# Top-k attention and two MLPs on one core: the mask of the scores as a PReLU on ScalarE

## The chip, the core and the metric

One core of a Trainium2 chip runs the whole program in one launch. The core has five engines that run side by side, each through its own list of instructions in the order in which they stand there: TensorE (PE in the profile; its weight loads are PEld), VectorE (DVE), ScalarE (ACT), GpSimd (POOL), and SyncE (SP), which issues most of the transfers. An instruction starts when those ahead of it on its engine are done with it and the semaphores that it waits for are set. The metric is the device time of one execution in microseconds (us).

## What is computed

Attention over 2 x 8 heads with 576 positions of 64 elements, in which each query keeps its 32 largest scores, and behind it two MLPs over the 1152 tokens. Cut to what matters:

```python
scores = scale * np.matmul(q, k.transpose(0, 1, 3, 2))
kth = np.partition(scores, -top_k, axis=-1)[..., -top_k:-top_k + 1]   # top_k = 32
scores = np.where(scores >= kth, scores, -1000000000.0)
scores = scores - np.max(scores, axis=-1, keepdims=True)
attn = np.exp(scores)
attn = attn / (np.sum(attn, axis=-1, keepdims=True) + 1e-09)
x = np.matmul(attn, v)            # then (tokens, 512)
h = x @ w_in;  x = (h * tanh(softplus(h))) @ w_out      # MLP 1, 512 -> 2048 -> 512
h = x @ w_in2; x = (relu(h) ** 2) @ w_out2              # MLP 2
```

## The kernel before

The tokens go through in four rounds (`ROUNDS`) of 256, 320, 320 and 256. A round's attention is made for four pairs of heads, in tiles of 128 queries by 576 keys; there are 72 such tiles. While a later round's attention runs, TensorE does the MLPs of an earlier one in the places that are left.

A tile (`tile_of`) goes over the engines in turn. TensorE makes the scores, ScalarE copies them to `s`. VectorE finds the 32nd largest of each row (lines 477 to 482): a MAX8 gives the eight largest, MATCH_REPLACE8 strikes them out into `w`, and this is done until four groups of eight are found in `mx`. Then comes the mask: GpSimd makes `e` = -3e38 where a score is below the 32nd largest, else 0 (line 491), and adds `s` to it (line 493). ScalarE makes the bias `nm` (line 492) and takes the exponential of `e`, whose row sum it leaves in `acc`. TensorE transposes `e`, ScalarE copies that to `pt`. Two tiles (the two heads of a pair) or one make a unit. At a unit's end (`unit_end`, lines 529 to 536) the sums get a small constant on ScalarE, VectorE takes the reciprocal (line 531), and ScalarE spreads it to `r` (line 534). When all units of a pair are there, TensorE multiplies with the values (`px`, line 556), and VectorE scales (line 584) into the round's `x1`, with which the round's MLPs begin.

Beside it run these: the weights are converted once (`convert`: two activations, one VectorE instruction at line 686, a transfer to DRAM as `kept`). In round 0 the MLPs take `kept` as it is (256 fp32 matmuls at line 774). In round 1 each of 32 pieces is split into a high and a low part: ScalarE casts, and GpSimd makes the low part with four subtractions (`wide`, line 260). Both are written to DRAM (`both`), from where rounds 2 and 3 take them. In rounds 1 to 3 every product is three matmuls, 768 instructions a round, and the activation `g` is split too (`gl`, line 253), on VectorE in round 1 and on GpSimd in rounds 2 and 3 (`GL = "gvggg"`). Round 0's and round 1's Mish shares ScalarE with the attention's exponentials, and a switch of function costs an ACT_TABLE_LOAD.

The order of each engine's instructions is not written out by hand. `Order` is a planner: every step of every process states its engine, its estimated time and a rank, and the planner lets the engine that comes free take the ready step of the lowest rank. What it decides is the program's order. So an estimate that changes moves instructions on all engines. A switch of the activation function has a price in the plan only where a step names its table, as the exponential and Mish do:

```python
        yield ("POOL", 1.0, 8, lambda: nc.gpsimd.tensor_scalar(out=e, in0=s, scalar1=mx[:, 3, 7:8], scalar2=LOWEST, op0=ALU.is_lt, op1=ALU.mult))
```

Here 1.0 is the estimated time in us and 8 the rank.

## Time and profile before

| | |
|---|---|
| median of 3 runs | 789.98 us (789.24 to 790.78) |
| the profiled execution | 789.56 us, of which the span of the profile is 787.4 us |
| busy, us (share of the span) | PE 657 (83%), PEld 578 (73%), DVE 483 (61%), ACT 482 (61%), POOL 449 (57%) |
| granted TensorE clock, mean | 0.93 of full speed |

The busy share is a mean over stages that have different limits. Up to about 143 us there is only attention and the conversion of weights, up to about 330 us round 0's MLPs run beside attention, up to about 567 us round 1's, and behind that TensorE has rounds 2 and 3 to itself. The views by stage say more than the table.

### The profile page before, as it was taken

The page shows a single profiled execution, that of the slowest core. Times are in us where ns is not written, and L with a number is a line of the kernel's source. Part 1 is how long each engine was busy: PE and PEld are TensorE (multiplying, and loading weights), DVE is VectorE, ACT ScalarE, POOL GpSimd, SP SyncE. Part 2 cuts the span into 40 slices and gives each one's busy share as a digit, 9 for nine tenths or more (in the row PEclk, how much of TensorE's full clock was granted, in tenths as well). Part 3 has the DMA queues.
Part 4 walks back from the last instruction along what each step waited for, and adds up shares of the span by engine and source line. Part 5 has one row for each costly group of instructions (what it writes and reads, how often), then busy time and mean ns, then how long its engine had stood idle before and what let it go on. Part 6 is the DMA issues. An engine that isn't in the chain of part 4 may idle for free.

```text
span 787.4 us, 11662 instructions
## 1 busy us (share of the span) xinstructions
PE 657.4 (83%) x4056; PEld 578.1 (73%) x4056; DVE 483.1 (61%) x889; ACT 481.7 (61%) x1015; POOL 449.2 (57%) x381
## 2 busy tenths in 40 slices
PE   5353554979996999797869789789899999999997
PEld 2242443767775887687668677678799999999997
DVE  3678999978986999999788879888200000100000
ACT  3677865799876984686785567874552073151550
POOL 2476567445535666979899899989642042041230
PEclk9997656999998999898999999999999999999999
DMA  7999921595999875566556565657888888889995
GB/s 200 281 372 268 323 66 32 206 350 174 351 320 354 261 250 157 182 216 255 192 218 206 191 206 215 263 201 269 291 282 313 288 294 288 311 323 357 369 354 202
DMA packets 95290, 201.83 MB, mean 256 GB/s; under 512 B 36352, under 2 KB 61440, under 8 KB 82944
## 3 DMA queue, kind: packets, MB, share of 16 engines
q1 hardware_dynamic: 94144, 200.83, 74.0%
q8 instruction: 32, 0.52, 0.3%
q10 hardware_dynamic: 1088, 0.26, 0.1%
q14 instruction: 26, 0.21, 0.1%
HBM read 146.01 MB, written 52.69 MB: 252 GB/s over the span
## 4 chain that ended last, share of the span: by engine, by line
PE 41%; POOL 17%; DMA 15%; DVE 12%; ACT 8%; issue 5%; SPq 1%; POOLq 0%; ACTq 0%
PE pm L774 32%; POOL wt L260 7%; POOL e L491 6%; DMA wt<-both 6%; DMA w<-kept 5%; DVE w L481 5%; DVE mx L482 4%; POOL e L493 3%; PE ps L464 3%; PE px L556 2%; DMA kept<-cu 2%; ACT L247 2%; PE pt L502 2%; DVE mx L478 1%; ACT e L247 1%
## 5 line engine op out<-in xcount | busy, mean ns | idle before, releaser
L491 POOL TENSOR_SCALAR e<-s,mx 128x576 f32<-128x576 f32 x72 | 163.1, 2267 | 115.8 <-DVE mx L482 82.3
L774 PE MATMUL pm<-gh,wt 128*128 128x320 f32 (+1 forms) x768 | 172.0, 308 | 3.3 <-ACT gh L247 1.5
L774 PE MATMUL pm<-xh,wt 128*128 128x320 f32 (+1 forms) x768 | 172.1, 310 | 2.8 <-DMA wt<-both 1.4
L482 DVE MAX8 mx<-w 128x8 f32<-128x576 f32 x216 | 164.4, 761 | 7.4
L774 PEld LDWEIGHTS pm<-xh,wt 128*128 128x128 f32 x768 | 130.7, 194 | 5.4 <-ACT h L247 2.2
L253 POOL TENSOR_TENSOR gl<-h,gh 128x320 fp32r<-128x320 f32 (+1 forms) x64 | 51.8, 809 | 144.8 <-ACT gh L247 110.2
L774 PEld LDWEIGHTS pm<-gh,wt 128*128 128x128 f32 x768 | 130.4, 193 | 5.4 <-DMA wt<-both 2.4
L774 PE MATMUL pm<-gl,wt 128*128 128x320 f32 (+1 forms) x384 | 117.5, 306 | 2.3 <-DVE gl L253 2.3
L774 PE MATMUL pm<-xl,wt 128*128 128x320 f32 (+1 forms) x384 | 117.5, 306 | 0.2
L481 DVE MATCH_REPLACE8 w<-mx,w 128x576 f32<-128x576 f32 x144 | 106.9, 742 | 0.0
L493 POOL TENSOR_TENSOR e<-s,e 128x576 f32<-128x576 f32 x72 | 104.0, 1447 | 3.8
L260 POOL TENSOR_TENSOR wt<-w,wt 128x256 fp32r<-128x256 f32 x128 | 94.6, 775 | 9.0 <-ACT wt L247 8.8
L502 PE MATMUL pt<-ident,e 128*128 128x128 f32 x288 | 53.0, 315 | 51.7 <-ACT e L247 41.1
L247 ACT ACTIVATE e<-e,nm 128x576 f32<-128x576 f32 x72 | 55.7, 774 | 66.0 <-POOL e L493 65.8
L502 PEld LDWEIGHTS pt<-ident,e 128*128 128x128 f32 x288 | 39.3, 160 | 61.8 <-ACT e L247 46.3
L774 PEld LDWEIGHTS pm<-gl,wt 128*128 128x128 f32 x384 | 74.2, 193 | 3.0 <-DVE gl L253 3.0
L774 PEld LDWEIGHTS pm<-xl,wt 128*128 128x128 f32 x384 | 74.7, 195 | 0.6 <-DVE xl L253 0.6
L247 ACT ACTIVATE h<-pm 128x320 f32<-128x320 f32 (+1 forms) x112 | 45.5, 413 | 46.4 <-PE pm L774 44.8
L955 DVE COPY ot<-pm 128x256 f32<-128x256 f32 x16 | 6.7, 421 | 101.9 <-PE pm L947 54.2
L253 DVE TENSOR_TENSOR xl<-pm,xh 128x320 fp32r<-128x320 f32 (+1 forms) x12 | 5.6, 468 | 101.7 <-ACT xh L247 101.5
L247 ACT ACTIVATE pt<-pt 128x640 f32<-128x640 f32 x72 | 50.4, 700 | 26.4 <-PE pt L504 25.9
L774 PE MATMUL pm<-gh,w 128*128 128x256 f32 x256 | 61.6, 385 | 1.2 <-DMA w<-kept 1.2
(94 smaller groups left out, 1175.5 us busy)
## 6 DMA issues: line engine op xcount, KB each, us to landing
wt<-both SPq DMA_DIRECT2D x64, 1024.0 KB, 5.1
w<-kept SPq DMA_DIRECT2D x64, 512.0 KB, 6.0
both<-wt SPq DMA_DIRECT2D x32, 1024.0 KB, 4.8
kept<-cu SPq DMA_DIRECT2D x32, 512.0 KB, 7.0
raw<-in_moe_w_in SPq DMA_DIRECT2D x9, 1024.0 KB, 9.0
raw<-in_moe_w_out SPq DMA_DIRECT2D x9, 1024.0 KB, 7.6
stage<-in_moe_w_in SPq DMA_DIRECT2D x7, 1024.0 KB, 8.6
stage<-in_moe_w_out SPq DMA_DIRECT2D x7, 1024.0 KB, 10.0
```

The lines of the kernel that those rows point to most:

```text
L247: op = ("ACT", t, rank, lambda: nc.scalar.activation(out, in_, func, **kw))
L253: return ({"g": "POOL", "v": "DVE"}[e], t, rank, lambda: eng.tensor_tensor(out=out, in0=in0, in1=in1, op=ALU.subtract))
L260: yield ("POOL", 0.05 + 0.0024 * n, rank, lambda: nc.gpsimd.tensor_tensor(out=out[:, z], in0=in0[:, z], in1=in1[:, z], op=op))
L464: nc.tensor.matmul(sp[:, i, 0:HK], q_, k_[:, i * HK:(i + 1) * HK], start=l == 0, stop=l == len(steps) - 1)
L478: nc.vector.max(out=mx[:, 0, :], in_=s)
L481: nc.vector.match_replace(out=w, in_to_replace=mx[:, i - 1, :], in_values=s if i == 1 else w, imm_value=LOWEST)
L482: nc.vector.max(out=mx[:, i, :], in_=w)
L491: yield ("POOL", 1.0, 8, lambda: nc.gpsimd.tensor_scalar(out=e, in0=s, scalar1=mx[:, 3, 7:8], scalar2=LOWEST, op0=ALU.is_lt, op1=ALU.mult))
L493: yield ("POOL", 1.4, 8, lambda: nc.gpsimd.tensor_tensor(out=e, in0=s, in1=e, op=ALU.add))
L502: nc.tensor.transpose(pp[:, c * P:(c + 1) * P], e[:, c * P:(c + 1) * P], ident)
L556: nc.tensor.matmul(xo[a * D:(a + 1) * D, 0:n], vt[z, a, c, :], pt[z, a, c, 0:n], start=c == 0, stop=c == NK)
L774: nc.tensor.matmul(o, w[a], x[b], start=first and i == 0, stop=last and i == len(terms) - 1)
```

## The change

The mask is no longer made on GpSimd. ScalarE makes it with a PReLU of (score - 32nd largest) x 2^40 with the slope 2^120 for negative values: what is kept stays as it is, what is not becomes very negative. The exponential then takes that with the scale divided by 2^40. The two biases that this needs are made by GpSimd on one element a row each; so are the small constant on the sums and the spread of the reciprocals for units of two tiles, which ScalarE did before. `s` is given free behind the PReLU.

```diff
-        nm = sb.tile([P, 1], F32, tag="nm", bufs=6, name="nm")
+        nm = sb.tile([P, 2], F32, tag="nm", bufs=6, name="nm")
...
-        yield ("POOL", 1.0, 8, lambda: nc.gpsimd.tensor_scalar(out=e, in0=s, scalar1=mx[:, 3, 7:8], scalar2=LOWEST, op0=ALU.is_lt, op1=ALU.mult))
-        yield act(0.22, 7, nm, mx[:, 0, 0:1], scale=-scale)
-        yield ("POOL", 1.4, 8, lambda: nc.gpsimd.tensor_tensor(out=e, in0=s, in1=e, op=ALU.add))
+        thr = mx[:, 3, 7:8]
+
+        def biases():
+            nc.gpsimd.tensor_scalar(out=nm[:, 0:1], in0=thr, scalar1=-UP, scalar2=None, op0=ALU.mult)
+            nc.gpsimd.tensor_scalar(out=nm[:, 1:2], in0=thr, scalar1=mx[:, 0, 0:1], scalar2=scale, op0=ALU.subtract, op1=ALU.mult)
+
+        yield ("POOL", 0.4, 1, biases)
+
+        yield act(0.78, 8, e, s, AF.Prelu, bias=nm[:, 0:1], scale=UP, alpha=2.0 ** 120)
         give("s")
-        yield act(0.85, 8, e, e, AF.Exp, "exp", bias=nm, scale=scale, accum_out=acc[:, a:a + 1])
+        yield act(0.85, 8, e, e, AF.Exp, "exp", bias=nm[:, 1:2], scale=scale / UP, accum_out=acc[:, a:a + 1])
...
-        yield act(0.22, 9, z, z, bias=1e-9)
+        yield ("POOL", 0.2, 1, lambda: nc.gpsimd.tensor_scalar(out=z, in0=z, scalar1=1e-9, scalar2=None, op0=ALU.add))
         yield ("DVE", 0.16, 3, lambda: nc.vector.reciprocal(z, z))
         if j < 2:
-            for a in range(2):
-                yield act(0.25, 10, r_[:, a, :], one.to_broadcast([P, D]), scale=acc[:, a:a + 1])
+            sums = acc[:, 0:2].rearrange("p (a o) -> p a o", o=1).to_broadcast([P, 2, D])
+            yield ("POOL", 0.4, 1, lambda: nc.gpsimd.tensor_tensor(out=r_, in0=sums, in1=one2, op=ALU.mult))
         else:
-            yield act(0.25, 10, r_, same, scale=z)
+            yield act(0.3, 10, r_, same, scale=z)
```

Since the estimates change, the planner puts the program into another order. Three places of it follow; lines of the changed kernel stand 2 to 7 higher than those of the one before.

On GpSimd in round 1, before: the subtractions of the weights (`wt`, line 260) stand between the masks of the tiles (lines 491 and 493).

```order
L260 TENSOR_TENSOR wt<-w,wt 128x256 x10
L491 TENSOR_SCALAR e<-s,mx 128x576 x2
L493 TENSOR_TENSOR e<-s,e 128x576 x2
L491 TENSOR_SCALAR e<-s,mx 128x576
L493 TENSOR_TENSOR e<-s,e 128x576
```

The like stretch of the changed kernel, where line 262 is the subtraction of the weights, lines 495 and 496 are the two biases, and line 537 the constant on a unit's sums:

```order
L262 TENSOR_TENSOR wt<-w,wt 128x256 x4
L495 TENSOR_SCALAR nm<-mx 128x1
L496 TENSOR_SCALAR nm<-mx 128x1
L262 TENSOR_TENSOR wt<-w,wt 128x256 x3
L537 TENSOR_SCALAR acc<-acc 128x1
L262 TENSOR_TENSOR wt<-w,wt 128x256
```

What stands between the subtractions has gone from 576 elements a row to one.

On VectorE in round 0, before: from the last MAX8 of a unit's second tile (its `mx_603`) to the unit's reciprocal (`acc_409`); the rows between are the next tiles' (`mx_663`, `mx_713`).

```order
L482 MAX mx_603<-w_602 128x8
L478 MAX mx_663<-s_576 128x8
L481 MATCH_REPLACE w_662<-mx_663,s_576 128x576
L482 MAX mx_663<-w_662 128x8
L481 MATCH_REPLACE w_662<-mx_663,w_662 128x576
L482 MAX mx_663<-w_662 128x8
L481 MATCH_REPLACE w_662<-mx_663,w_662 128x576
L482 MAX mx_663<-w_662 128x8
L478 MAX mx_713<-s_618 128x8
L531 RECIPROCAL acc_409<-acc_409 128x2
```

The same unit in the changed kernel, where the tile is `mx_605` and the sums are `acc_401`:

```order
L484 MAX mx_605<-w_604 128x8
L480 MAX mx_659<-s_573 128x8
L483 MATCH_REPLACE w_658<-mx_659,s_573 128x576
L484 MAX mx_659<-w_658 128x8
L483 MATCH_REPLACE w_658<-mx_659,w_658 128x576
L484 MAX mx_659<-w_658 128x8
L538 RECIPROCAL acc_401<-acc_401 128x2
```

The reciprocal stands three rows nearer to the tile whose sums it takes. All 40 reciprocals move like this; most have the five rows of here between, some three.

On ScalarE at the start of round 0's MLPs, before: Mish of the MLP (`gh`), a conversion (`cu`), and the exponential (`e_1174`), with the table loads between them.

```order
L247 ACTIVATE gh_1082<-pm_1164 128x256
L247 ACT_TABLE_LOAD
L247 ACTIVATE cu_1170<-stage_88 128x1024
L247 ACT_TABLE_LOAD
L247 ACTIVATE gh_1082<-pm_1188 128x256
L247 ACTIVATE s_1203<-ps_1103 128x576
L247 ACT_TABLE_LOAD
L247 ACTIVATE e_1174,acc_878<-e_1174,nm_1010 128x576
```

In the changed kernel the first instruction of this piece is an exponential, and the PReLU (`e_1170` from `s_941`) stands alone between two Mish instructions:

```order
L249 ACTIVATE e_1122,acc_786<-e_1122,nm_968 128x576
L249 ACT_TABLE_LOAD
L249 ACTIVATE gh_1065<-pm_1137 128x256
L249 ACT_TABLE_LOAD
L249 ACTIVATE e_1170<-s_941,nm_1017 128x576
L249 ACT_TABLE_LOAD
L249 ACTIVATE gh_1065<-pm_1149 128x256
L249 ACTIVATE s_1192<-ps_1147 128x576
```

The PReLU needs a table load on either side there, which its step's estimate doesn't contain. In the whole program there are 28 loads before (16 in round 0's MLPs, 10 in round 1's) and 34 after (18 and 14). On TensorE, of the 2560 matmuls at line 774 (774 before, 781 after), 1006 stand ahead of the last pair's `px` before, and 952 after.

## Rows read from the trace of the kernel before

**Rows 1.** The page's chain of work that ended last, by line

```profile
PE pm L774 32%; POOL wt L260 7%; POOL e L491 6%; DMA wt<-both 6%; DMA w<-kept 5%; DVE w L481 5%; DVE mx L482 4%; POOL e L493 3%; PE ps L464 3%; PE px L556 2%; DMA kept<-cu 2%; ACT L247 2%; PE pt L502 2%; DVE mx L478 1%; ACT e L247 1%
```

**Rows 2.** Windows: stretch, its length, busy us (instructions) by engine, clock, DMA

```profile
0.00:145.00 145.00, 75.57 (x327) 53.08 (x328) 115.46 (x206) 92.09 (x177) 82.73 (x61) 0.80 0.68 209
145.00:300.00 155.00, 141.85 (x739) 117.76 (x738) 133.89 (x227) 130.16 (x254) 78.92 (x48) 0.96 0.86 294
300.00:555.40 255.40, 217.16 (x1344) 189.00 (x1342) 221.18 (x424) 174.24 (x387) 227.38 (x202) 0.93 0.61 215
567.00:787.40 220.40, 212.35 (x1576) 209.16 (x1575) 11.81 (x31) 80.08 (x187) 51.79 (x64) 1.00 0.85 308
```

**Rows 3.** Groups of GpSimd, 300 to 555.4 us

```profile
L260 POOL TENSOR_TENSOR wt<-w,wt 128x256 fp32r<-128x256 f32 x122 | 90.4, 777 | 9.0 <-ACT wt L247 8.8 <-ACT nm L247 0.2
L491 POOL TENSOR_SCALAR e<-s,mx 128x576 f32<-128x576 f32 x35 | 78.8, 2253 | 17.3 <-DVE acc L531 5.4 <-DVE mx L482 5.0 <-ACT y L247 2.0
L493 POOL TENSOR_TENSOR e<-s,e 128x576 f32<-128x576 f32 x35 | 49.7, 1425 | 1.3
```

**Rows 4.** Waits of VectorE, 300 to 555.4 us: us, times, longest

```profile
DVE acc L531 <- ACT acc L247: 16.0, 11, 2.8
DVE mx L478 <- ACT acc L247: 4.9, 1, 4.9
```

**Rows 5.** A group of VectorE, 300 to 555.4 us

```profile
L253 DVE TENSOR_TENSOR gl<-h,gh 128x320 fp32r<-128x320 f32 x32 | 22.7, 740 | 2.8 <-ACT gh L247 2.7
```

**Rows 6.** A group of VectorE, 567 to 787.4 us

```profile
L253 DVE TENSOR_TENSOR xl<-x,xh 128x320 fp32r<-128x320 f32 x4 | 1.7, 487 | 2.6 <-ACT xh L247 2.6
```

**Rows 7.** Line 686: two groups, 0 to 145 us; then its least, median and most

```profile
L686 DVE SCALAR_TENSOR_TENSOR cu<-cu,raw 128x1024 int32<-128x1024 int32 x7 | 10.9, 1552 | 6.0 <-ACT raw L247 6.0
L686 DVE SCALAR_TENSOR_TENSOR cu<-cu,stage 128x1024 int32<-128x1024 int32 x6 | 8.1, 1354 | 1.6 <-ACT stage L247 1.6
...
L686 DVE SCALAR_TENSOR_TENSOR cu<-cu,raw x18: 1207/1229/2425, 32.4 to 270.8; 128x1024 int32<-128x1024 int32 x18
```

**Rows 8.** Groups of ScalarE, whole span

```profile
L247 ACT ACTIVATE e<-e,nm 128x576 f32<-128x576 f32 x72 | 55.7, 774 | 66.0 <-POOL e L493 65.8
L247 ACT ACT_TABLE_LOAD x27 | 34.6, 1283 | 0.5
L247 ACT ACTIVATE r<-one,acc 128x64 f32<-128x64 f32 x64 | 19.5, 340 | 1.7 <-DVE acc L531 1.7
L247 ACT ACTIVATE nm<-mx 128x1 f32<-128x1 f32 x72 | 14.0, 196 | 0.0
```

**Rows 9.** Timeline of round 0's last tile: start, us, engine, line, operation

```profile
128.09 0.76 DVE L482 MAX8 mx<-w 128x8 f32<-128x576 f32 x1
129.74 0.76 DVE L482 MAX8 mx<-w 128x8 f32<-128x576 f32 x1
...
130.67 2.21 POOL L491 TENSOR_SCALAR e<-s,mx 128x576 f32<-128x576 f32 x1 [1.15 <-DVE mx L482]
132.96 1.40 POOL L493 TENSOR_TENSOR e<-s,e 128x576 f32<-128x576 f32 x1
134.40 0.77 ACT L247 ACTIVATE e<-e,nm 128x576 f32<-128x576 f32 x1 [1.76 <-POOL e L493]
135.08 0.19 ACT L247 ACTIVATION_READ_ACCUMULATOR e<-e,nm 128x1 f32 x1
```

**Rows 10.** Small instructions of GpSimd, whole span

```profile
L253 POOL TENSOR_TENSOR qd0l<-kc,qd0h 128x128 fp32r<-128x128 f32 x4 | 1.8, 454 | 6.8 <-ACT kc L247 6.8
L233 POOL MEMSET one<- 128x1 f32 x1 | 0.1, 98 | 0.0
```

**Rows 11.** Timeline of the last round's last tile

```profile
554.62 0.76 DVE L482 MAX8 mx<-w 128x8 f32<-128x576 f32 x1
557.34 2.21 POOL L491 TENSOR_SCALAR e<-s,mx 128x576 f32<-128x576 f32 x1
561.11 0.78 ACT L247 ACTIVATE e<-e,nm 128x576 f32<-128x576 f32 x1 [2.39 <-POOL e L493]
```

More of the change, by code (lines that the diff above doesn't have):

```diff
@@ L18 @@
 LOWEST = -3.0e38
+UP = 2.0 ** 40
 LOW3 = 2.0 ** -29 * (1.0 - 2.0 ** -12)
@@ L233, in topk_attention_two_mlps @@
     nc.gpsimd.memset(one, 1.0)
+    one2 = one.rearrange("p (a o) -> p a o", a=1).to_broadcast([P, 2, D])
     same = cst.tile([P, 2, 64], F32, name="same")
```

## The prediction

> **What bounds the kernel now.** I began with the chain of work that ended last, grouped by line [rows 1]. The reader is to see two things there. TensorE's products at line 774 are the largest item, 32%. GpSimd is the second, and three of its lines are on the chain: the low parts of the weights (line 260, 7%) and the two mask instructions (lines 491 and 493, 6% and 3%). The change takes away the last two, 9% of 787 us or some 70 us of chain. That is no gain yet: what is next behind them decides.
>
> So I split the span by stage [rows 2]. Behind 567 us TensorE is busy for 212.4 of 220.4 us, at full clock and without attention. Nothing can be won there: an earlier start only moves this stretch. From 145 to 300 us TensorE is busy for 141.9 of 155 us and ScalarE for 130.2. The idle time of TensorE lies in the first 145 us, where it has no MLP yet, and from 300 to 555 us: 38 of 255.4 us. In this third stretch GpSimd is busy for 227.4 us, and in its groups [rows 3] the masks of 35 tiles take 78.8 + 49.7 = 128.5 us, the weights 90.4. VectorE comes next with 221.2 of 255.4 us. Its waits [rows 4] show what the other 34.2 us are: 16.0 + 4.9 = 20.9 us for the sums `acc`, which come out of the chain mask, exponential, constant. So in this stretch GpSimd makes VectorE late, and VectorE's tiles set the end of attention.
>
> **What a tile costs.** On GpSimd a tile loses 2.25 + 1.43 us [rows 3] and gets two instructions on one element a row, b each. A unit gets b more for the constant and a spread of 128 elements. No row shows a TENSOR_SCALAR on one element. From below it is bounded by the MEMSET of one element, 0.10 us, and for the spread there is the subtraction of 128 elements, 0.45 us [rows 10]. From above: subtracting what 576 elements cost in the two-operand form, (1.425 - 0.454)/448 = 2.2 ns each or 1.25 us, from the mask's 2.25 us leaves 1.0 us that might be a price per instruction. I take 0.2 us, since the line through the 128 and 576 element rows leaves 0.17 us for an instruction as such; both ends go into the range.
>
> On ScalarE a tile gets the PReLU. It has the exponential's shape and also a bias from a tile, so 0.77 us [rows 8], and loses the bias `nm`, 0.20 us. A unit of two tiles loses the constant (of `nm`'s kind, 0.20) and two spreads of 0.34. That is 1.55 - 0.39 - 0.20 - 0.68 = +0.28 us for a unit. ScalarE hardly gets more to do.
>
> **The path of a unit.** In the timeline of round 0's last tile [rows 9] GpSimd starts 0.17 us behind the last MAX8, which ends at 130.50, and the exponential starts at 134.40, 0.04 us behind the mask. So mask and hops are 3.90 us. In the change they are 0.17 + 2b + 0.04 + 0.77 = 1.38 us at b = 0.2. Behind the exponential the sum is read 0.87 us after its start; with the same hops the reciprocal can start 2.06 + 3b = 2.66 us after the tile's last MAX8. VectorE's order gives it a MAX8 and two further steps of 1.65 us (128.09 to 129.74), 0.76 + 3.3 = 4.1 us, at most of the 40 units. So the nearer place of the reciprocal costs nothing while b is under 0.68 and ScalarE takes the PReLU without a queue of more than 1.4 us. If that cover is gone, VectorE stands still, and behind the reciprocal stand the next tiles' MAX8 and MATCH_REPLACE8, for which everything in attention waits.
>
> **The sum, by stage.**
>
> First stretch: the last tile of round 0 lies on the path to `x1`, so 3.90 - 1.38 = 2.5 us. VectorE's line 686 took 1.55 us seven times and 1.35 six times, with a median of 1.23 [rows 7]; the longer ones fell beside masks on GpSimd. 7 x 0.32 + 6 x 0.12 = 3.0 us go with the masks. Together -5.5.
>
> Second stretch: TensorE and ScalarE bind it, not GpSimd. About ten units lie there (72 tiles less the third stretch's 35, and half of the rest), so ScalarE gets 2.8 us more, and two more table loads of 1.28 us: the PReLU can need a load on either side where Mish runs. Of these 5.4 us I take half, since ScalarE is idle for 25 of 155 us: +2.7.
>
> The Trainium skill's page "ScalarE: Activation LUTs", section "What ACT_TABLE_LOAD costs", gives 2.66 us for every switch, 1.28 for the load and 1.38 for a drain. The rows have 1.283 us, and 0.5 us of idle time in all before 27 loads; by the page's price the sum would come out 4 us higher. I keep the rows' price.
>
> Third stretch: VectorE's 221.2 us lose what GpSimd's masks cost it. Its subtraction of 320 elements takes 0.740 us here [rows 5] and 0.487 us behind 567 us, where GpSimd has no masks [rows 6]: 32 x 0.253 = 8.1 us, so 213.1. (The weights' subtractions go on, so part of this may stay; the cost to the sum is at most 8.) Of its 34.2 us idle, 20.9 are the waits for sums. Between 0, as the 4.1 us allow, and 20.9 as now I take 6, a third of a microsecond for each of some 19 units, because ScalarE runs in order and its queue varies. So 13.3 + 6 = 19.3. Four more table loads are 5.1 us; half of it, 2.6. That makes 235.0 us in place of 255.4: -20.4. TensorE's work of 217.2 us has room in it, and less than that has to be done, as follows.
>
> End of attention: from the last MAX8 (555.38) to the exponential (561.11) are 5.73 us, with a piece of the weights ahead of the mask [rows 11]. 5.73 - 1.38 = -4.4.
>
> What is pushed behind: 54 fewer matmuls of line 774 stand ahead of the last `px`. TensorE does them in the last stretch, at 212.35/1576 = 0.135 us each: +7.3.
>
> Sum: -5.5 + 2.7 - 20.4 - 4.4 + 7.3 = -20.3 us. The profiled execution took 789.56 us (2.2 us beside its span, kept as they are), so 769.3 us; the median of the runs is 0.4 us higher, so 769.5 us.
>
> Its own range: without waits for sums and loads on the path the third stretch is 226.4 us and the whole 758; with half of the waits, 10.5, and the loads in full it is 242 and the whole 779. If VectorE were never idle there, 213.1, the whole would be 745.
>
> **The rivals.** *The waits are halved, no more* (20.9 to between 11 and 17 us), as other queues than GpSimd's hold the sums back as well. For it speaks that even in the first stretch, where GpSimd is busy for 83 of 145 us only, VectorE is idle for 29. Then 779 to 788 us.
>
> *ScalarE takes GpSimd's place.* The mask now stands in ScalarE's order, between Mish and casts, and the PReLU can bring loads with it that its estimate leaves out. If sums come as late as now, the third stretch is 213.1 + 34.2 + 5.1 = 252.4 us, the second takes the full +5.4, the end one load more (-3.1): -5.5 + 5.4 - 3.0 - 3.1 + 7.3 = +1.1, or 791 us, no change or slower. The 54 matmuls pushed behind then cost what the stretch doesn't win. Against it: ScalarE is busy for 174 of 255 us there. The same page's section "Table sets: the hidden batching unit" would have activations batched by set, which speaks against this change; in the rows that would be six loads, 7.7 us, at most.
>
> *The small GpSimd instructions are dear.* At b = 1.0 the reciprocal can start 5.06 us after the MAX8, 0.96 us too late at each unit. First stretch: -5.5 + 1.6 for the path + 8 x 0.96 = +3.8; second: 2.7 + half of 13 x 0.96 = +8.9; third: 213.1 + 13.3 + 18 + 2.6 = 247, or -8.4; end -2.8; behind +7.3: together +9, 798 us, slower. It decides from about b = 0.9. Against it: the subtraction of 128 elements, with two operands, takes 0.45 us in all.
>
> **Chances.** The forecast with its own range 0.57; halved waits 0.21; ScalarE in GpSimd's place 0.12 (785 to 797); dear instructions 0.10. Under 0.2% (1.6 us) a measurement of this kernel can't be told from no change. Faster: the first two and a little of the third, 0.80; same 0.06; slower 0.14. The range of 753 to 791 us reaches from below the forecast's own end, where a little of the 745 case lies, into the third case, and leaves out the fourth.
>
> **What will show it.** Right: GpSimd's busy time falls from 449 us by 267 and gains 144 + 40 instructions of 0.2 and 32 of some 0.45, to about 235; the PReLU takes 0.77 us; VectorE's waits for sums from 300 us on fall under 10 us, its 320-element subtraction to about 0.5; the last MAX8 moves from 554.6 to about 530 us; behind the last `px` TensorE is as dense as now. Wrong: a TENSOR_SCALAR on one element over 0.7 us; long waits of RECIPROCAL for GpSimd, or of the PReLU's followers for loads; TensorE idle as long as before from 300 us to the last `px`; or weights from DRAM that come late once attention ends sooner.

## The result and the profile after

The changed kernel takes 771.33 us, median of 4 runs (770.26 to 773.01), beside 790.28 us (789.24 to 790.78) for the kernel before: a ratio of 0.976 with a 95% interval of 0.974 to 0.979. The forecast was 769.5. The profiled execution took 773.01 us, with a span of 771.2.

The page of the changed kernel: busy time by engine, then the chain that ended last, by line ([rows 1] of before).

```profile
PE 649.1 (84%) x4056; PEld 569.3 (74%) x4056; DVE 470.1 (61%) x889; ACT 513.1 (67%) x917; POOL 249.2 (32%) x453
...
PE pm L781 33%; DMA w<-kept 8%; DMA wt<-both 5%; DVE w L483 4%; POOL wt L262 4%; DVE mx L484 4%; ACT e L249 3%; ACT L249 3%; PE ps L466 3%; SPq L311 2%; PE px L563 2%; ACT wt L249 2%; DMA kt<-in_k 1%; PE pt L509 1%; DMA raw<-in_moe_w_in 1%
```

GpSimd has 200 us less to do, and the mask's 9% of the chain are gone. But the span fell by 16 us, not by 70. In the masks' place stand items that had been shorter or absent: the loads of `kept` (5 to 8%), ScalarE's exponentials and its table loads (`ACT L249`, 3%).

Windows of the changed kernel, cut at the stages of [rows 2] as they now lie; columns as there.

```profile
0.00:141.00 141.00, 79.73 (x337) 54.89 (x337) 114.28 (x204) 99.71 (x153) 34.05 (x75) 0.75 0.71 216
141.00:300.00 159.00, 137.82 (x720) 112.57 (x718) 124.75 (x226) 135.34 (x226) 27.31 (x68) 0.97 0.82 275
300.00:531.30 231.30, 202.05 (x1314) 177.90 (x1312) 217.81 (x425) 191.69 (x345) 124.89 (x228) 0.95 0.67 229
531.30:541.50 10.20, 9.32 (x63) 7.28 (x64) 1.15 (x4) 5.39 (x9) 8.52 (x15) 1.00 0.82 312
541.50:771.20 229.70, 220.19 (x1629) 216.68 (x1627) 12.14 (x33) 80.92 (x188) 54.44 (x68) 1.00 0.86 311
```

The third stretch does the same 35 tiles in 231.3 us that took 255.4, and VectorE is now busy for 217.8 of them (94%, before 87%). Behind 541.5 us TensorE is as dense as before, but that stretch is longer: 54 more matmuls were left for it. Across 141 to 300 us the share of VectorE is 78%; there it waits.

Waits of VectorE in the changed kernel: first from 0 to 141 us, then 141 to 300, then 300 to 531.3 ([rows 4] has the last of them before).

```profile
DVE acc L538 <- POOL acc L537: 4.7, 2, 3.4
...
DVE acc L538 <- POOL acc L537: 21.2, 10, 6.4
...
DVE acc L538 <- POOL acc L537: 3.9, 4, 2.0
```

From 300 us on the waits for sums fell from 20.9 to 3.9 us, as forecast (6). In the second stretch they rose, from 2.6 us before to 21.2. One of the 20.9 us needs a word: 4.9 of them stand ahead of a MAX8, which takes no sum.

```profile
395.02 0.76 DVE L478 MAX8 mx<-s 128x8 f32<-128x576 f32 x1 [4.85 <-ACT acc L247]
```

It needs a copy of scores, which ScalarE made at 394.29 us behind two exponentials that had waited for their masks. So the mask is behind this wait too, but waits for sums alone fell from 16.0 to 3.9 us. Summed over the whole span they did not fall at all (25.1 us before, 30.5 now): they moved from the third stretch to the second. There TensorE is now idle for 21.2 of 159 us, where it was idle for 13.2 of 155, so they are not free there.

Groups of GpSimd and ScalarE, whole span, changed kernel ([rows 3, 8, 10]).

```profile
L262 POOL TENSOR_TENSOR wt<-w,wt 128x256 fp32r<-128x256 f32 x128 | 91.6, 742 | 35.9 <-ACT wt L249 30.2 <-PE pt L511 2.1 <-POOL wt L262 1.3
L496 POOL TENSOR_SCALAR nm<-mx 128x1 f32<-128x1 f32 x72 | 26.0, 361 | 0.0
L495 POOL TENSOR_SCALAR nm<-mx 128x1 f32<-128x1 f32 x72 | 25.1, 349 | 127.9 <-DVE mx L484 127.6
L541 POOL TENSOR_TENSOR r<-acc,one 128x128 f32<-128x128 f32 x32 | 13.0, 407 | 20.9 <-DVE acc L538 18.4 <-PE ps L466 1.6 <-PE pt L338 0.9
L537 POOL TENSOR_SCALAR acc<-acc 128x2 f32<-128x2 f32 x32 | 7.4, 232 | 59.8 <-ACT e L249 59.3
...
L249 ACT ACTIVATE e<-s,nm 128x576 f32<-128x576 f32 x72 | 55.6, 772 | 14.5 <-POOL nm L495 14.0
L249 ACT ACT_TABLE_LOAD x33 | 42.3, 1283 | 1.0 <-DMA kept<-cu 0.4
```

An instruction on one or two elements a row takes 0.23 to 0.36 us on average; the PReLU takes the forecast 0.77; the table loads are 33, the six more that were counted.

Two timelines of the changed kernel follow, each row as start, duration, engine, line, operation. The first is round 0's last tile ([rows 9] of before).

```profile
132.12 0.76 DVE L484 MAX8 mx<-w 128x8 f32<-128x576 f32 x1
...
133.04 0.21 POOL L495 TENSOR_SCALAR nm<-mx 128x1 f32<-128x1 f32 x1 [1.20 <-DVE mx L484]
133.23 0.30 POOL L496 TENSOR_SCALAR nm<-mx 128x1 f32<-128x1 f32 x1
133.29 0.77 ACT L249 ACTIVATE e<-s,nm 128x576 f32<-128x576 f32 x1 [1.75 <-POOL nm L495]
134.16 0.78 ACT L249 ACTIVATE e<-e,nm 128x576 f32<-128x576 f32 x1
...
137.43 0.42 DVE L591 TENSOR_TENSOR x<-px,inv 128x256 f32<-128x256 f32 x1 [0.59 <-ACT inv L249]
```

From the end of the MAX8 (132.88) to the exponential are 1.28 us, where 3.90 were, so the forecast's 1.38 was nearly right. The PReLU even starts behind the first bias; the second is made beside it.

The second is in the middle of round 0's Mish, ScalarE against the sums, and it is the worst of the ten waits from 141 to 300 us but one.

```profile
149.24 0.76 ACT L249 ACTIVATE e<-s,nm 128x576 f32<-128x576 f32 x1
150.02 1.28 ACT L249 ACT_TABLE_LOAD   x1
151.31 0.38 ACT L249 ACTIVATE gh<-pm 128x256 f32<-128x256 f32 x1
151.59 0.65 ACT L249 ACTIVATE s<-ps 128x576 f32<-128x576 f32 x1
152.25 1.28 ACT L249 ACT_TABLE_LOAD   x1
153.55 0.78 ACT L249 ACTIVATE e<-e,nm 128x576 f32<-128x576 f32 x1
...
154.50 0.23 POOL L537 TENSOR_SCALAR acc<-acc 128x2 f32<-128x2 f32 x1 [8.45 <-ACT e L249]
154.76 0.17 DVE L538 RECIPROCAL acc<-acc 128x2 f32<-128x2 f32 x1 [4.56 <-POOL acc L537]
```

Between the PReLU and its own exponential ScalarE's order has a Mish with a load on either side and a copy of scores. The exponential comes 3.5 us behind the PReLU and VectorE stands still for 4.56 us.

**The stages against the forecast.** The marks are VectorE's scaling that ends round 0's and round 1's attention (137.43 and 307.06 us; before 143.21 and 309.03), the end of the last MAX8 (531.27; before 555.38), the last scaling (541.13; before 567.28), and the end of the span.

| stage | forecast | measured |
|---|---|---|
| first stretch, to round 0's last scaling | -5.5 | -5.8 |
| second, to round 1's | +2.7 | +3.8 |
| third, to the last MAX8 | -20.4 | -22.1 |
| end of attention | -4.4 | -2.0 |
| work pushed behind | +7.3 | +9.9 |
| sum, spans of the profiled executions | -20.3 | -16.2 |

The medians are 19.0 us apart. So far this agrees. The experiments ask whether it agrees for the reasons given: the theory is that lifting the masks off GpSimd makes the sums early and that attention then ends early. The rival is that the new estimates gave the planner another order, and that the order is the gain.

### The profile page after: what moved, and what is told of

The parts are those of the page before. It is cut to its first block, busy times and chain, and to the rows that moved or that the text cites. A ratio compares the mean times of both kernels' runs of the same rounds, so it can differ in the third digit from the quotient of the medians.

```text
span 771.2 us, 11656 instructions
## 1 busy us (share of the span) xinstructions
PE 649.1 (84%) x4056; PEld 569.3 (74%) x4056; DVE 470.1 (61%) x889; ACT 513.1 (67%) x917; POOL 249.2 (32%) x453
## 4 chain that ended last, share of the span: by engine, by line
PE 41%; DMA 22%; ACT 14%; DVE 11%; POOL 5%; SPq 4%; issue 2%; ACTq 0%; POOLq 0%; DVEq 0%
PE pm L781 33%; DMA w<-kept 8%; DMA wt<-both 5%; DVE w L483 4%; POOL wt L262 4%; DVE mx L484 4%; ACT e L249 3%; ACT L249 3%; PE ps L466 3%; SPq L311 2%; PE px L563 2%; ACT wt L249 2%; DMA kt<-in_k 1%; PE pt L509 1%; DMA raw<-in_moe_w_in 1%
## 5 line engine op out<-in xcount | busy, mean ns | idle before, releaser
L781 PE MATMUL pm<-xh,wt 128*128 128x320 f32 (+1 forms) x768 | 170.1, 308 | 2.9 <-DMA wt<-both 1.7
L781 PE MATMUL pm<-gh,wt 128*128 128x320 f32 (+1 forms) x768 | 166.0, 302 | 3.3 <-DMA wt<-both 1.2
L781 PEld LDWEIGHTS pm<-gh,wt 128*128 128x128 f32 x768 | 126.7, 188 | 4.5 <-DMA wt<-both 2.2
L781 PE MATMUL pm<-gl,wt 128*128 128x320 f32 (+1 forms) x384 | 115.1, 300 | 0.0
L262 POOL TENSOR_TENSOR wt<-w,wt 128x256 fp32r<-128x256 f32 x128 | 91.6, 742 | 35.9 <-ACT wt L249 30.2
L509 PE MATMUL pt<-ident,e 128*128 128x128 f32 x288 | 50.7, 305 | 43.0 <-ACT e L249 23.6
L509 PEld LDWEIGHTS pt<-ident,e 128*128 128x128 f32 x288 | 37.5, 154 | 53.2 <-ACT e L249 27.4
L249 ACT ACTIVATE h<-pm 128x320 f32<-128x320 f32 (+1 forms) x112 | 45.2, 413 | 45.8 <-PE pm L781 41.8
L781 PEld LDWEIGHTS pm<-gl,wt 128*128 128x128 f32 x384 | 72.3, 188 | 0.1
L249 ACT ACTIVATE pt<-pt 128x640 f32<-128x640 f32 x72 | 50.4, 700 | 28.3 <-PE pt L511 27.9
L495 POOL TENSOR_SCALAR nm<-mx 128x1 f32<-128x1 f32 x72 | 25.1, 349 | 127.9 <-DVE mx L484 127.6
L249 ACT ACTIVATE e<-s,nm 128x576 f32<-128x576 f32 x72 | 55.6, 772 | 14.5 <-POOL nm L495 14.0
L249 ACT ACTIVATE e<-e,nm 128x576 f32<-128x576 f32 x72 | 55.8, 776 | 6.4 <-POOL nm L496 0.5
```

Source lines behind the costliest of these rows:

```text
L249: op = ("ACT", t, rank, lambda: nc.scalar.activation(out, in_, func, **kw))
L262: yield ("POOL", 0.05 + 0.0024 * n, rank, lambda: nc.gpsimd.tensor_tensor(out=out[:, z], in0=in0[:, z], in1=in1[:, z], op=op))
L495: nc.gpsimd.tensor_scalar(out=nm[:, 0:1], in0=thr, scalar1=-UP, scalar2=None, op0=ALU.mult)
L509: nc.tensor.transpose(pp[:, c * P:(c + 1) * P], e[:, c * P:(c + 1) * P], ident)
L781: nc.tensor.matmul(o, w[a], x[b], start=first and i == 0, stop=last and i == len(terms) - 1)
```

## The experiments

No kernel here leaves out or changes part of what is computed. Ratios are to the kernel before on the same chip, with 95% intervals.

| kernel | us (median, range) | ratio |
|---|---|---|
| changed kernel | 771.33 (770.26 to 773.01) | 0.976 [0.974, 0.979] |
| e1 old work, honest mask estimates | 777.98 (773.77 to 779.2) | 0.981 [0.977, 0.985] |
| e2 mask alone, planned anew | 794.06 (789.49 to 799.59) | 1.003 [0.999, 1.007] |
| e3 constant and spread alone, planned anew | 790.49 (788.05 to 793.06) | 1.000 [0.997, 1.002] |
| e4 PReLU's table named | 776.98 (770.98 to 781.89) | 0.980 [0.974, 0.987] |
| f1 old work in the new order | 881.21 (878.53 to 882.55) | 1.113 [1.110, 1.117] |
| f3 new work in the old order | 776.89 (774.08 to 785.67) | 0.984 [0.978, 0.991] |
| f4 mask alone in the old order | 773.89 (771.57 to 776.18) | 0.980 [0.977, 0.983] |
| p1 one estimate 0.04 us higher, new work | 778.04 (774.62 to 783.45) | 0.985 [0.980, 0.989] |
| p2 one estimate 0.05 us higher, old work | 794.65 (793.26 to 798.85) | 1.006 [1.003, 1.010] |
| f5 the biases three times | 792.4 (788.88 to 796.88) | 1.002 [0.999, 1.005] |
| g1 planned by measured durations | 759.03 (757.95 to 759.38) | 0.961 [0.959, 0.963] |
| g2 the same, further estimates | 743.99 (740.82 to 747.1) | 0.942 [0.937, 0.947] |

**e1.** The kernel before, with only the two mask estimates set to what the trace shows.

```diff
-        yield ("POOL", 1.0, 8, lambda: nc.gpsimd.tensor_scalar(out=e, in0=s, ...
+        yield ("POOL", 2.25, 8, lambda: nc.gpsimd.tensor_scalar(out=e, in0=s, ...
-        yield ("POOL", 1.4, 8, lambda: nc.gpsimd.tensor_tensor(out=e, in0=s, in1=e, ...
+        yield ("POOL", 1.45, 8, lambda: nc.gpsimd.tensor_tensor(out=e, in0=s, in1=e, ...
```

> The kernel before with nothing but the two estimates of the masks set to what the trace had (2.25 and 1.45 us in place of 1.0 and 1.4): the same work on every engine, in another order. If the gain is the work lifted from GpSimd, GpSimd stays the engine that makes the sums late from 300 us on, and the time stays within 6 us of 790 (784 to 796). If the gain is the better plan, in which masks stand where they really fall, most of it comes here too: 770 to 780 us.

That is the second case: on its chip 13 us (791.05 to 777.98) come without a single instruction lifted from GpSimd, which is busy for 447 us as before. So a time of some 775 us is no proof that the masks were the cost; the rival stays in.

**e2.** Only the mask is moved; constant and spread stay on ScalarE with their old estimates.

```diff
-        yield ("POOL", 0.2, 1, lambda: nc.gpsimd.tensor_scalar(out=z, in0=z, scalar1=1e-9, ...
+        yield act(0.22, 9, z, z, bias=1e-9)
...
-            yield ("POOL", 0.4, 1, lambda: nc.gpsimd.tensor_tensor(out=r_, in0=sums, in1=one2, op=ALU.mult))
+            for a in range(2):
+                yield act(0.25, 10, r_[:, a, :], one.to_broadcast([P, D]), scale=acc[:, a:a + 1])
```

> The changed kernel with the constant on the sums and the spread of the reciprocals back on ScalarE (40 x 0.20 + 64 x 0.34 = 30 us more there, GpSimd 22 us less). If the mask is the gain, most of it stays: 771 to 778 us. If ScalarE is now so tight that what it is spared by the second half of the change pays for the PReLU, 30 us more on it in the stretches where it is 85% busy bring the time to 780 to 788 us.

No gain, and a time above both expected ranges. It brings a new reading. Windows of this kernel, cut at its last product with the values, `px`, and columns as before:

```profile
0.00:541.10 541.10, 416.82 (x2314) 342.45 (x2316) 458.25 (x850) 443.99 (x825) 162.82 (x296) 0.90 0.69 227
541.10:791.00 249.90, 237.93 (x1744) 232.83 (x1740) 15.74 (x40) 87.22 (x197) 67.54 (x86) 1.00 0.86 315
```

The changed kernel, cut at its own last `px`:

```profile
0.00:539.70 539.70, 427.11 (x2418) 351.09 (x2418) 457.62 (x856) 431.34 (x728) 193.13 (x383) 0.90 0.73 241
539.70:771.20 231.50, 221.99 (x1642) 218.22 (x1638) 12.51 (x33) 81.71 (x189) 56.09 (x71) 1.00 0.86 311
```

Attention ends at the same time in both (541.1 and 539.7 us), and yet the spans are 20 us apart. In e2 TensorE has done 104 instructions fewer by then (2314 and 2418); 96 of them are MLP matmuls, and they follow behind. So the end of attention alone does not set the time. Of the 20 us, 11.7 are TensorE's idle time ahead of the last `px` (541.1 - 416.8 = 124.3 us in e2, 112.6 in the changed kernel), 5.6 are its busy time for the same 4056 instructions (654.7 and 649.1 us), and 2.5 are idle time behind.

**e3.** Only constant and spread go to GpSimd, with the estimates of the change; the mask stays.

```diff
-        yield act(0.22, 9, z, z, bias=1e-9)
+        yield ("POOL", 0.2, 1, lambda: nc.gpsimd.tensor_scalar(out=z, in0=z, scalar1=1e-9, ...
...
-            for a in range(2):
-                yield act(0.25, 10, r_[:, a, :], one.to_broadcast([P, D]), scale=acc[:, a:a + 1])
+            yield ("POOL", 0.4, 1, lambda: nc.gpsimd.tensor_tensor(out=r_, in0=sums, in1=one2, op=ALU.mult))
```

> The kernel before with only the constant and the spread on GpSimd, the masks as before. If GpSimd's load is the bound, 22 us more on it (40 x 0.23 + 32 x 0.41) win nothing: 788 to 800 us. If the relief of ScalarE is the gain, 780 us or less.

No difference. Halves that bring nothing alone (e2, e3) and 19 us together would be odd if it were the work; all three were planned anew, so work and order are mixed in them.

**e4.** The PReLU names the exponential's table, so that the planner counts its loads.

```diff
-        yield act(0.78, 8, e, s, AF.Prelu, bias=nm[:, 0:1], scale=UP, alpha=2.0 ** 120)
+        yield act(0.78, 8, e, s, AF.Prelu, "exp", bias=nm[:, 0:1], scale=UP, alpha=2.0 ** 120)
```

> The changed kernel, the PReLU's step naming the exponential's table, so that the plan charges a switch for it; 26 table loads in place of 34. If the loads that the plan left out cost time where Mish runs (round 0's MLPs got 5 us slower relative to the start than before), 764 to 768 us. If the loads are beside the path and the waits there come of ScalarE's queue in general, 769 to 774 us.

25 loads stand in the group instead of 33, 10.3 us less for ScalarE, and the time is not lower: at 777 us it lies above both expected ranges, though the intervals of the ratios overlap. The Trainium skill's page "ScalarE: Activation LUTs", section "Table sets: the hidden batching unit", would have activations batched by set; here fewer loads bought nothing that can be measured (e4 was planned anew, and a gain of less than the scatter that p1 and p2 show would not be seen). Nor did 41 loads make f4, below, slow.

**f1 and f3.** These separate work and order. f1 issues the old instructions in the steps of the new plan; f3 issues the new ones in the steps and with the estimates of the old plan. TensorE's and VectorE's orders are, instruction for instruction, those of the changed kernel in f1 and those of the kernel before in f3. f1, its core:

```diff
-            nc.gpsimd.tensor_scalar(out=nm[:, 0:1], in0=thr, scalar1=-UP, ...
-            nc.gpsimd.tensor_scalar(out=nm[:, 1:2], in0=thr, scalar1=mx[:, 0, 0:1], ...
+            nc.gpsimd.tensor_scalar(out=e, in0=s, scalar1=thr, scalar2=LOWEST, op0=ALU.is_lt, op1=ALU.mult)
+            nc.gpsimd.tensor_tensor(out=e, in0=s, in1=e, op=ALU.add)
...
-        yield act(0.78, 8, e, s, AF.Prelu, bias=nm[:, 0:1], scale=UP, alpha=2.0 ** 120)
+        yield act(0.78, 8, nm[:, 0:1], mx[:, 0, 0:1], scale=-scale)
```

> The changed kernel's plan, with the old instructions put into its steps: both masks where the biases stood, the old bias where the PReLU stood, constant and spread on ScalarE. TensorE's and VectorE's orders are those of the changed kernel, row for row; 24 table loads. If the lifted work is the gain, the masks come late in a plan that gives them 0.4 us, and the time is 790 us or more (3.2 us more on each unit's path, of which a margin of 1.4 us hides a part). If the order is the gain, 771 to 780 us.

f3, its core, against the changed kernel:

```diff
-        yield ("POOL", 0.4, 1, biases)
-        yield act(0.78, 8, e, s, AF.Prelu, bias=nm[:, 0:1], scale=UP, alpha=2.0 ** 120)
+        yield ("POOL", 1.0, 8, biases)
+        yield act(0.22, 7, e, s, AF.Prelu, bias=nm[:, 0:1], scale=UP, alpha=2.0 ** 120)
+        yield ("POOL", 1.4, 8, lambda: None)
...
-            yield ("POOL", 0.4, 1, lambda: nc.gpsimd.tensor_tensor(out=r_, in0=sums, in1=one2, op=ALU.mult))
+            yield ("ACT", 0.25, 10, lambda: nc.gpsimd.tensor_tensor(out=r_, in0=sums, in1=one2, op=ALU.mult))
+            yield ("ACT", 0.25, 10, lambda: None)
```

> The plan of the kernel before, with the new instructions put into its steps: biases where the first mask stood, the PReLU where the old bias stood, nothing where the second mask stood, constant and spread on GpSimd. TensorE's and VectorE's orders are those of the kernel before, row for row; 42 table loads, 14 more than before (18 us of ScalarE, part of it on the path). If the lifted work is the gain, 768 to 778 us in spite of the loads. If the order is the gain, 785 to 795 us.

The waits of f1, whole span:

```profile
ACT e L249 <- POOL e L496: 184.8, 63, 5.8
...
DVE acc L538 <- ACT acc L537: 91.8, 40, 6.9
```

The four corners are 790 (old work, old order), 777 (new work, old order), 881 (old work, new order) and 771 (both new). The order is no gain for the old work: it costs 91 us, because it places the reciprocals for a short mask, and now VectorE waits at all 40 units. In the old order the new work brings 13 us. There the sums are early in the third stretch, as the theory has it: VectorE waits for them for 2.7 us in f3 and 2.3 us in f4 (below), where the kernel before has 16.0 [rows 4], and the last MAX8 starts at 545.9 and 542.4 us instead of 554.6. Their rows, f3 from 300 to 547 us and f4 from 300 to 543.2:

```profile
DVE acc L539 <- POOL acc L538: 2.7, 3, 1.4
...
DVE acc L539 <- ACT acc L249: 2.3, 3, 1.1
```

So the lifted masks are a cause by themselves, and the rival, that the order is the gain, falls. Whether the new order adds something to the new work can't be told: the intervals of f3 and of the changed kernel meet at 0.978 to 0.979.

**f4.** f3 with constant and spread on ScalarE as before: the mask alone, in the old order.

```diff
-        yield ("ACT", 0.22, 9, lambda: nc.gpsimd.tensor_scalar(out=z, in0=z, scalar1=1e-9, ...
+        yield act(0.22, 9, z, z, bias=1e-9)
...
-            yield ("ACT", 0.25, 10, lambda: nc.gpsimd.tensor_tensor(out=r_, in0=sums, in1=one2, op=ALU.mult))
-            yield ("ACT", 0.25, 10, lambda: None)
+            for a in range(2):
+                yield act(0.25, 10, r_[:, a, :], one.to_broadcast([P, D]), scale=acc[:, a:a + 1])
```

> The new mask alone in the plan of the kernel before (as the new work in the old order, but with the constant and the spread on ScalarE, 30 us more there); TensorE's and VectorE's orders row for row those of the kernel before, 42 table loads. If the mask is the gain and the 794 us of the mask alone with a plan of its own came of that plan, 774 to 782 us. If ScalarE can't carry PReLU and spreads together, 785 to 795 us.

0.980, 17 us faster on its chip: the mask is all of the gain that can be measured. The half of the change that takes constant and spread to GpSimd is worth nothing in the old order, and e3 says the same of it beside the old masks.

**p1 and p2.** How much does planning anew scatter? One estimate is moved a little; the same instructions are issued in another order.

```diff
-        yield act(0.78, 8, e, s, AF.Prelu, bias=nm[:, 0:1], scale=UP, alpha=2.0 ** 120)
+        yield act(0.82, 8, e, s, AF.Prelu, bias=nm[:, 0:1], scale=UP, alpha=2.0 ** 120)
```

> The changed kernel with the estimate of the PReLU at 0.82 us in place of 0.78: the same instructions, planned anew. If work sets the time, 769 to 774 us. If the time hangs on which plan comes out, it moves by more than 5 us either way.

```diff
-        yield ("POOL", 1.4, 8, lambda: nc.gpsimd.tensor_tensor(out=e, in0=s, in1=e, op=ALU.add))
+        yield ("POOL", 1.45, 8, lambda: nc.gpsimd.tensor_tensor(out=e, in0=s, in1=e, op=ALU.add))
```

> The kernel before with the estimate of the second mask at 1.45 us in place of 1.4: the same instructions, planned anew. If work sets the time, 787 to 793 us, and the 778 us that both true estimates gave came of their truth. If the time hangs on which plan comes out, it moves by more than 5 us.

0.8% and 0.6% slower, 6.7 us (from the changed kernel's median) and 4.7 us (on its chip; just under what its expectation called a move), for 0.04 and 0.05 us in an estimate. A difference of this size between two kernels that were planned apart (the changed kernel and p1, e4 or f3) says nothing about their work. The 20 us that e2 lost are more than this scatter showed, but they too came with the order: f4 has e2's work, and in the old order it gains.

**f5.** The margin of the forecast: does a small delay on the path of a unit cost nothing up to some 1.4 us? The two biases are made three times, about 1.0 us more for a tile (GpSimd's busy time rises by 70.0 us over 72 tiles), and the plan is untouched.

```diff
+            for _ in range(3):
                 nc.gpsimd.tensor_scalar(out=nm[:, 0:1], in0=thr, scalar1=-UP, ...
                 nc.gpsimd.tensor_scalar(out=nm[:, 1:2], in0=thr, scalar1=mx[:, 0, 0:1], ...
```

> The changed kernel with the two biases of each tile made three times over (4 x 0.26 = 1.0 us more on the path of every tile, 75 us more of GpSimd), plan and orders unchanged. If a margin of some 1.3 us lies between the sums and the reciprocals, as forecast, the time moves by less than 4 us (769 to 775). If the margin is gone already, as the 30 us of waits for sums may mean, most of 40 x 1.0 us comes through: 785 us or more.

Its waits, whole span:

```profile
DVE acc L539 <- POOL acc L538: 40.7, 30, 4.6
...
PE ps L466 <- ACT s L249: 48.1, 29, 4.9
```

21 us slower than the changed kernel, all of the gain. VectorE waits for sums 30 times instead of 17 and for 40.7 us instead of 30.5, and TensorE waits for the copies of scores 48.1 us instead of 39.8. The last scaling is at 564.98 us instead of 541.13: a third of a microsecond late for each tile, out of one. Not all of that is waiting: ahead of the last `px` TensorE is idle for 10 us more and busy for 13 us more with the same instructions (see the table below). And f5 does not separate the longer path from GpSimd's 70 us of added work. Either way the margin is not there at many units.

**g1.** What do honest estimates bring the changed kernel? Estimates that the trace contradicts are set near to what it shows, and the PReLU names its table. (One of them, the PReLU's 0.69, goes the other way: its rows show 0.77.)

```diff
-        eng, t = {"g": (nc.gpsimd, 0.1 + 0.0023 * n), "v": (nc.vector, 0.2 + 0.0012 * n)}[e]
+        eng, t = {"g": (nc.gpsimd, 0.1 + 0.0023 * n), "v": (nc.vector, 0.28 + 0.0012 * n)}[e]
-            yield ("POOL", 0.05 + 0.0024 * n, rank, ...
+            yield ("POOL", 0.74, rank, ...
-        yield ("POOL", 0.4, 1, biases)
+        yield ("POOL", 0.55, 1, biases)
-        yield act(0.78, 8, e, s, AF.Prelu, bias=...
+        yield act(0.69, 8, e, s, AF.Prelu, "exp", bias=...
-        yield ("POOL", 0.2, 1, lambda: nc.gpsimd.tensor_scalar(out=z, in0=z, ...
+        yield ("POOL", 0.25, 1, lambda: nc.gpsimd.tensor_scalar(out=z, in0=z, ...
-        yield ("DVE", 1.65, lambda: 15 if x1_done[0].done or i < EARLY else 25, ...
+        yield ("DVE", 1.24, lambda: 15 if x1_done[0].done or i < EARLY else 25, ...
```

> The changed kernel planned with what its trace had: biases 0.55, PReLU 0.69 with the exponential's table, constant 0.25, the weights' subtractions 0.74, VectorE's subtraction 0.08 higher, its conversion 1.24 in place of 1.65; 24 table loads. If true estimates are worth time, as for the masks of the kernel before, 755 to 767 us. If a new plan is a new draw, 768 to 780.

**g2.** g1 with four more estimates corrected: GpSimd's subtractions, the exponential, the copy of `pt` and the spread.

```diff
-        eng, t = {"g": (nc.gpsimd, 0.1 + 0.0023 * n), "v": ...
+        eng, t = {"g": (nc.gpsimd, 0.2 + 0.0021 * n), "v": ...
-        yield act(0.85, 8, e, e, AF.Exp, "exp", ...
+        yield act(0.87, 8, e, e, AF.Exp, "exp", ...
-            yield act(0.75, 10, pt[:, a, :, j * P:(j + 1) * P], x)
+            yield act(0.70, 10, pt[:, a, :, j * P:(j + 1) * P], x)
-            yield ("POOL", 0.4, 1, lambda: nc.gpsimd.tensor_tensor(out=r_, in0=sums, ...
+            yield ("POOL", 0.41, 1, lambda: nc.gpsimd.tensor_tensor(out=r_, in0=sums, ...
```

> The kernel with measured estimates (759 us) planned once more, with five further estimates set to its trace (GpSimd's subtractions 0.2 + 0.0021 a column, the copy of the transposed tile 0.70, the exponential 0.87, the spread 0.41), the same instructions. If true estimates are what that kernel won by, 754 to 765 us. If its 759 us was a good draw among plans, anything from 762 to 778.

759 and 744 us, 12 and 27 us less than the changed kernel, with the same arithmetic on the same engines. g1 lies in its first range; g2 lies below both of its ranges, so neither of the two readings foresaw it. Windows of g2, cut at its last `px`, then its waits for sums over the whole span:

```profile
0.00:515.40 515.40, 425.22 (x2440) 355.07 (x2442) 457.55 (x856) 418.01 (x719) 195.08 (x385) 0.92 0.76 254
515.40:740.70 225.30, 217.55 (x1618) 214.64 (x1614) 12.42 (x33) 81.17 (x188) 54.62 (x68) 1.00 0.85 315
...
DVE acc L538 <- POOL acc L537: 9.0, 8, 1.9
```

Attention ends 24 us earlier than in the changed kernel and 22 TensorE instructions more are done by then, and VectorE waits for sums 9.0 us instead of 30.5. Part of g2's 15 us on g1 may be scatter of the size that p1 and p2 show; g1 and g2 were not varied further.

**The rows side by side.** Ahead of the last `px`, and from it on (us; idle is the stretch ahead of the last `px` less TensorE's busy time in it):

| kernel | last `px` | TensorE busy ahead of it | idle ahead of it | MLP matmuls behind it | time behind it |
|---|---|---|---|---|---|
| before | 565.8 | 443.8 | 122.0 | 1554 | 221.6 |
| f3 | 555.4 | 442.3 | 113.1 | 1554 | 221.7 |
| f4 | 552.3 | 441.1 | 111.2 | 1554 | 220.7 |
| changed | 539.7 | 427.1 | 112.6 | 1608 | 231.5 |
| f5 | 563.5 | 440.6 | 122.9 | 1608 | 230.1 |
| f1 | 649.8 | 460.7 | 189.1 | 1608 | 231.0 |
| e1 | 578.9 | 460.1 | 118.8 | 1404 | 198.5 |
| e2 | 541.1 | 416.8 | 124.3 | 1704 | 249.9 |
| g1 | 518.3 | 419.4 | 98.9 | 1632 | 238.6 |
| g2 | 515.4 | 425.2 | 90.2 | 1584 | 225.3 |

The first three have one order on TensorE, and so have the next three. Within such a group the time behind the last `px` is the same to 1.4 us; what differs lies ahead of it.

The time behind the last `px` is 0.141 to 0.147 us for each matmul left, in every kernel. e1 shows most plainly that the end of attention alone misleads: it ends 13 us later than before, and the span is 10 us shorter, with 150 matmuls more done beside attention.

TensorE's busy time is no constant either. The changed kernel, f5 and f1 do the same instructions in the same order, and ahead of the last `px` the busy time rises with the idle time, while the mean granted clock of that stretch falls: 0.90, 0.88 and 0.85 of full speed. So the last `px` came later there by more than the added idle time. Of the 16.2 us between the spans of before and changed, 9.4 are idle time ahead of the last `px`, 8.3 are busy time for the same 4056 instructions (657.4 and 649.1 us), and 1.5 are lost behind it; in e1 busy time is 6.5 of the 10. What makes up the busy part between kernels of different orders was not tested.

## Why the prediction was right, and where it was not

The time, its sign and most terms were right, and f3 and f4 show that the mechanism named is real: in an unchanged order the lifted mask gains 17 us alone (f4) and 13 us with constant and spread (f3). That the median came within 2 us of the forecast is luck in part. The sum by stage misses the profiled spans by 4.1 us, and p1 shows that the same work planned anew moves by 6.7 us, which nothing in the sum could foresee.

*What bounds the kernel.* That GpSimd's masks make VectorE late from 300 us on was right: the waits for sums there fell to 3.9 us and the last MAX8 came 24.1 us earlier, where the terms of the first three stages give 23.2. That "VectorE's tiles set the end of attention" is right as well, but the step from there to the time is short of a part: e2 ends attention as early and gains nothing. The forecast had the part in its last term, the 54 matmuls pushed behind, and took their count from the order; without that count the sum would have been -27.6 us, where the profiled spans show -16.2 and the medians -19.0.

*The first stretch* was right in sum: -5.8 for -5.5. Line 686, now 693, takes 1.28 and 1.22 us in its two groups (before 1.55 and 1.35, [rows 7]), and the path is 1.28 us for the forecast 1.38.

*The second stretch* gave back 3.8 us for 2.7. The rival "ScalarE takes GpSimd's place" was weighed for the third stretch above all and came true in this one: waits for sums of 21.2 us, PReLU and exponential apart with a load between them. So did a sign of being wrong that the prediction had named, long waits of RECIPROCAL for GpSimd (up to 6.4 us). The stage grew by less than that rival's 5.4 us, but the late sums were not free: between the marks TensorE was idle for 21.5 us, where it was idle for 13.3, and had 22 instructions fewer to do.

*The third stretch*, -22.1 for -20.4, is right by errors that cancel. The 320-element subtraction on VectorE fell from 0.740 us only to 0.659, not to 0.487: 2.6 us [rows 5] instead of the 8.1 that were reckoned. The forecast had named the reason, the weights that stay on GpSimd, as possible. The trace of before, taken instruction by instruction, shows that they were most of it from the start: 16 of the 32 subtractions lie beside those of the weights and take 0.86 us on average, nine lie beside the first mask instruction and take 0.50, and two have nothing beside them and take 0.48. Two stretches of it, three of VectorE's subtractions beside the mask and two beside the weights:

```profile
363.77 4.75 POOL L491 TENSOR_SCALAR e<-s,mx 128x576 f32<-128x576 f32 x2
365.18 1.28 DVE L253 TENSOR_TENSOR gl<-h,gh 128x320 fp32r<-128x320 f32 x3
...
510.11 1.96 DVE L253 TENSOR_TENSOR gl<-h,gh 128x320 fp32r<-128x320 f32 x2
510.74 1.93 POOL L260 TENSOR_TENSOR wt<-w,wt 128x256 fp32r<-128x256 f32 x2
```

So the step that laid the whole difference on the masks was wrong. A row of the changed kernel, 300 to 531.3 us:

```profile
L255 DVE TENSOR_TENSOR gl<-h,gh 128x320 fp32r<-128x320 f32 x32 | 19.9, 659 | 1.7 <-ACT gh L249 1.7
```

So VectorE stayed at 217.8 us busy, not 213.1, but its idle time was 13.5 us where 21.9 were reckoned. The forecast took half of the added loads as VectorE's waiting; e4 and f4 show no price for the loads that stands out of the scatter.

*The end of attention* gave 2.0 us, not 4.4. In the last tile GpSimd starts 1.17 us behind the MAX8 (531.27), not 0.17, since it still has subtractions of the weights to end, as it had before:

```profile
530.51 0.76 DVE L484 MAX8 mx<-w 128x8 f32<-128x576 f32 x1
532.44 0.22 POOL L495 TENSOR_SCALAR nm<-mx 128x1 f32<-128x1 f32 x1
...
533.56 0.78 ACT L249 ACTIVATE e<-e,nm 128x576 f32<-128x576 f32 x1
...
541.13 0.43 DVE L591 TENSOR_TENSOR x<-px,inv 128x256 f32<-128x256 f32 x1 [6.19 <-ACT inv L249]
```

That leaves 3.4 us of gain up to the exponential, and between it and the last scaling 7.6 us pass instead of 6.2.

*The work pushed behind* was 54 matmuls, as counted, and cost 9.9 us instead of 7.3: 0.18 us each in place of 0.135, of which 1.5 us in all are TensorE's idle time.

*The small instructions and their margin.* b was taken as 0.2 us; the medians are 0.22 and 0.30 and the means 0.35 and 0.36, so GpSimd is busy for 249 us, not 235. The step that failed is the margin, "costs nothing while b is under 0.68": f5 adds about 1.0 us to a tile's path, which is less than the 1.4 us claimed, and loses 21 us. In the changed kernel itself the reciprocals wait at 17 of the 40 units, for 30.5 us. Two things were wrong. First, the cover of 4.1 us was read off units with five rows of VectorE between the last MAX8 and the reciprocal. 22 units have five or more; 18 have three or fewer, and three rows are 0.76 + 1.65 = 2.4 us, less than the 2.66 us that the path was reckoned to take. In f5, 16 of these 18 wait, and 14 of the other 22. Second, the condition on ScalarE's queue, no more than 1.4 us, did not hold. Besides the Mish above, the longest wait shows it; its two biases were made at 285.41 us, and the PReLU then stood behind a copy that waited for TensorE:

```profile
292.73 0.70 ACT L249 ACTIVATE pt<-pt 128x640 f32<-128x640 f32 x1 [6.50 <-PE pt L511]
293.33 0.77 ACT L249 ACTIVATE e<-s,nm 128x576 f32<-128x576 f32 x1
...
295.39 0.16 DVE L538 RECIPROCAL acc<-acc 128x1 f32<-128x1 f32 x1 [6.38 <-POOL acc L537]
```

The places of the reciprocal that I read as cover are places in an order, taken at unhindered steps, and VectorE is not the only one to wait: in f5 TensorE's waits for the copies of scores, which stand among the PReLUs and exponentials on ScalarE, rose by 8.3 us.

*Constant and spread.* The path was reckoned with them on GpSimd, and nothing in the sum was claimed for them. f4 and e3 agree.

What stays open: whether the new order of the changed kernel is a little better or worse for its work than the old one. f3, f4 and the changed kernel lie within what a new plan scatters. Also open is how much of the gains of g1 and g2 belongs to estimates that are truer and how much to chance: no plan was made with estimates moved as far, but at random.

## What to carry to other kernels

Where a planner makes the order, an edit that changes estimates changes two things at once; issue the new instructions in the old order (and the old in the new) before you credit the edit. Read the gain at the engine that fills the tail: when the last dependent step ends and how much filler work is left by then, since either alone misleads (e1 ended later and was faster, e2 ended earlier and was not). And try the planner with estimates set to the trace's durations whenever an engine's work changes: here the three plans made so were 13, 12 and 27 us faster than those with the old estimates (e1, g1, g2), the last by more than the change itself (19), while p2, which sets one estimate to what the trace shows, cost 5 us, and p1, which moves one a little away from it, 7. That it is their truth that pays is not shown.
